# A causal convolution and a two-layer SiLU network on one core: transposes moved from the matmul engine to DMA, 192 channels packed as 128 + 128, a third PSUM buffer, and the second matmuls delayed by one chunk

## The chip, the cores and the metric

The kernel runs on one NeuronCore of a Trainium2 chip. The metric is the device time of one execution in microseconds (us). Most executions of one kernel agree within 0.3%. "Granted clock" is the PE clock in the profile, 1.00 at full speed. Engines are named as in the profile: PE is the matmul engine, PEld its weight loads, DVE the vector engine, ACT the scalar (activation) engine, SP the engine whose queue issues most DMAs.

## The reference, cut to what matters

```python
# x: (8, 4096, 192) f32, weight: (8 heads, 7 taps)
w = softmax(weight, axis=-1)
out = einsum('hk,bskhg->bshg', w, x_unf)     # causal 7-tap convolution along the sequence, per head of 24 channels
h = out.reshape(32768, 192) @ w_in           # (192, 2048)
g = h * (1 / (1 + exp(-beta * h)))           # beta: one number for each of the 2048 columns
return g @ w_out                             # (2048, 192)
```

## The kernel before

The 32768 tokens go in 32 chunks of 1024. The convolution wants channels on partitions, x comes with tokens on partitions, so x is cast to fp16, transposed on PE into PSUM (the memory that holds the results of the matmuls) and copied by DVE to SBUF (the on-chip memory that holds their operands). DVE then does 7 taps for each of two halves of 96 channels. "First matmuls" below are those that make `hpsum`, "second matmuls" those that make `opsum`.

```python
    ps_tr = ... bufs=2     # transposes, 2 KB a partition each
    ps_h  = ... bufs=2     # hpsum, 4 KB each
    ps_o  = ... bufs=2     # opsum, 1.5 KB each
    # ... weights are loaded and cast ...
    for c in range(nchunks):
        # ... 8 loads of x, 4 casts to fp16 on ACT ...
        for hh in range(2):
            tr = ps_tr.tile([128, NSUB // 2, 256], FP16)
            for si in range(NSUB // 2):
                s = hh * (NSUB // 2) + si
                nc.tensor.transpose(tr[0:DB, si, 0:SUB], x16[:, s, 0:DB], ident)
                nc.tensor.transpose(tr[0:DB, si, SUB:2 * SUB], x16[:, s, DB:D], ident)
            # ... two copies of tr into xt1 and xt2 on DVE ...
        # ... per half: tensor_scalar_mul, then 6 scalar_tensor_tensor on DVE; the last writes yt
        for fc in range(NFC):                          # 16 steps
            hpsum = ps_h.tile([128, CHUNK], FP32)
            # ... 4 first matmuls of 512 columns from win1/yt1 and win2/yt2 ...
            nc.scalar.activation(gt[:, fc, :], hpsum, AF.Silu, scale=beta_sb[:, fc:fc + 1])
        for sg in range(NSUB // 2):
            opsum = ps_o.tile([SUB, 2, D], FP32)
            # ... 2 x 16 second matmuls of 192 columns from gt and wout ...
            o_sb = opool.tile([SUB, 2, D], FP32)
            nc.scalar.copy(o_sb, opsum)
            # ... store ...
```

The instructions of each engine are put in order when the kernel is built, and this compiled order is not simply the program's. In the trace of the kernel before, second matmuls of a chunk are mixed into its own first ones, and transposes of later chunks stand at 485.9 us, ahead of a block of 98 second matmuls, and at 494.9 us, behind it.

## Time and profile before

| | before |
|---|---|
| median | 1036.39 us (12 runs) |
| PE, ACT, DVE busy | 904.2, 676.5, 544.3 us of 1033.7 |
| first and second matmuls a chunk | 64 of 512 columns, 128 of 192 columns |
| two chunks (485 to 547 us) | 62.3 us |
| dense PE time for one chunk (estimate, below) | 24.3 us |

From the page of the kernel before: busy time of each engine, the granted PE clock in 40 slices, and the chain of work that ended last.

```profile
PE 904.2 (87%) x6656; PEld 582.7 (56%) x6656; DVE 544.3 (53%) x719; ACT 676.5 (65%) x780; POOL 0.7 (0%) x6
...
PEclk9999999898998989989898998989989899998989
...
PE 68%; DVE 25%; ACT 4%; SPq 1%; DMA 1%; issue 0%; DVEq 0%; ACTq 0%
```

PE looks nearly full, but a quarter of the chain is DVE's: PE is held up at times. The granted clock dips too. The list of waits of the kernel before (who waited for whom, us in total, times, longest) says by what.

```profile
DVE xt L148 <- PE tr L146: 449.3, 17, 30.0
ACT o_sb L205 <- PE opsum L197: 175.9, 113, 2.2
...
ACT gt L188 <- PE hpsum L184: 130.5, 84, 8.3
PE hpsum L184 <- DVE yt L169: 99.7, 32, 10.0
```

DVE waits for PE's transposes, up to 30 us at a time, and PE then waits for DVE's convolution. Two engines wait for each other in turn. The PE timeline of the kernel before shows (start, us, engine, what, count; idle time before and what ended it in brackets):

```profile
501.71 1.01 PE L184 MATMUL hpsum<-yt,win 96*128 96x512 bf16 x2 [5.72 <-DVE yt L169]
502.91 4.29 PE L184 MATMUL hpsum<-yt,win 96*128 96x512 bf16 x10 [0.18 <-DVE yt L169]
```

After the wait of 5.72 us a first matmul takes about 430 ns, twice its later time; the granted clock is 0.50 from 501.7 to 504 us, 0.63 to 508 us and 1.00 after that (busy time by stretches). That is about 2.6 us lost each time (2.3 x 0.50 + 4.0 x 0.37). The trace has 15 such waits from 126 us on, one in every second chunk, so about 39 us in all, an estimate.

The next lines show two steps of an hpsum phase and, last, the block that ended the chunk before it.

```profile
534.24 1.02 PE L184 MATMUL hpsum<-yt,win 96*128 96x512 bf16 x4
535.10 0.41 PE L197 MATMUL opsum<-wout,gt 128*128 128x192 bf16 x3
535.47 1.02 PE L184 MATMUL hpsum<-yt,win 96*128 96x512 bf16 x4
536.33 0.25 PE L197 MATMUL opsum<-wout,gt 128*128 128x192 bf16 x1
536.47 1.02 PE L184 MATMUL hpsum<-yt,win 96*128 96x512 bf16 x4
...
522.91 8.26 PE L197 MATMUL opsum<-wout,gt 128*128 128x192 bf16 x98
```

Two steps take 2.23 us (534.24 to 536.47), 1.115 each, with 2 second matmuls a step on average. The other 98 of a chunk follow in a block at 82 ns each, 8.0 us. In such a block (523 to 531 us) ACT is busy for 2.6 of 8.0 us. At the same rate per column a first matmul takes about 215 ns, so PE's own work is 64 x 0.215 + 128 x 0.082 = 24.3 us a chunk, an estimate.

### The profile page before, as it was taken

How to read it: one execution, taken by the hardware profiler on the slowest of the kernel's cores; microseconds unless marked ns; L12 is line 12 of the kernel's file. 1: busy time of each engine (PE TensorE's matmuls, PEld its weight loads, DVE VectorE, ACT ScalarE, POOL GpSimd, SP SyncE). 2: the span in 40 equal slices, each digit the busy share in tenths (PEclk: the TensorE clock that was granted, in tenths of full speed). 3: DMA queues.
4: the chain of work that ended last, by engine and by line, in shares of the span. 5: the costliest groups of instructions: out<-in, count | busy, mean ns of one | idle time of the engine just before them, and what ended most of it. 6: DMA issues, size and time to landing. Idle time of an engine off the chain costs nothing.

```text
span 1033.7 us, 15639 instructions
## 1 busy us (share of the span) xinstructions
PE 904.2 (87%) x6656; PEld 582.7 (56%) x6656; DVE 544.3 (53%) x719; ACT 676.5 (65%) x780; POOL 0.7 (0%) x6
## 2 busy tenths in 40 slices
PE   1599799797998979799797997979899797997978
PEld 1266566365664656556465663656646465664655
DVE  6970653908448092661917538093571916529060
ACT  3777577674777747677575776747677474765735
POOL 0000000000000000000000000000000000000000
PEclk9999999898998989989898998989989899998989
DMA  6741301203021130301203021031200010010001
GB/s 170 195 125 32 92 21 48 56 31 93 31 62 31 32 92 32 85 16 37 79 31 93 23 62 39 31 92 32 62 2 31 31 32 31 16 32 16 31 31 32
DMA packets 77215, 54.52 MB, mean 53 GB/s; under 512 B 8792, under 2 KB 76376, under 8 KB 77144
## 3 DMA queue, kind: packets, MB, share of 16 engines
q1 hardware_dynamic: 77144, 53.52, 18.1%
q8 instruction: 52, 0.85, 0.3%
q14 instruction: 19, 0.16, 0.1%
HBM read 28.33 MB, written 25.17 MB: 52 GB/s over the span
## 4 chain that ended last, share of the span: by engine, by line
PE 68%; DVE 25%; ACT 4%; SPq 1%; DMA 1%; issue 0%; DVEq 0%; ACTq 0%
PE hpsum L184 46%; PE opsum L197 21%; DVE acc L169 18%; DVE yt L169 4%; ACT gt L188 3%; DVE acc L166 1%; DVE xt L148 1%; DVE xt L152 1%; SPq L121 1%; DMA x_sb<-in_x_dram 0%; DMA beta_sb<-in_moe_beta_dram 0%; PE tr L145 0%; PE tr L146 0%; ACT x L129 0%; DVE wout L112 0%
## 5 line engine op out<-in xcount | busy, mean ns | idle before, releaser
L188 ACT ACTIVATE gt<-hpsum,beta_sb 128x1024 bf16<-128x1024 f32 x512 | 552.0, 1113 | 148.1 <-PE hpsum L184 130.5
L184 PE MATMUL hpsum<-yt,win 96*128 96x512 bf16 x2048 | 559.2, 402 | 101.8 <-DVE yt L169 99.7
L197 PE MATMUL opsum<-wout,gt 128*128 128x192 bf16 x4096 | 422.7, 247 | 2.6 <-ACT gt L188 0.7
L197 PEld LDWEIGHTS <-gt 128*128 128x128 bf16 x4096 | 346.7, 98 | 105.2 <-ACT gt L188 19.8
L169 DVE SCALAR_TENSOR_TENSOR acc<-xt,wk,acc 96x1024 f16<-96x1024 f16 (+1 forms) x350 | 390.4, 1182 | 0.0
L184 PEld LDWEIGHTS <-win 96*128 96x128 bf16 x2048 | 205.5, 101 | 317.1 <-issue 158.9
L148 DVE COPY xt<-tr 96x512 f16<-96x512 f16 x64 | 26.5, 414 | 449.3 <-PE tr L146 449.3
L205 ACT COPY o_sb<-opsum 128x384 f32<-128x384 f32 x128 | 61.2, 478 | 178.2 <-PE opsum L197 175.9
L169 DVE SCALAR_TENSOR_TENSOR yt<-xt,wk,acc 96x1024 bf16<-96x1024 f16 (+1 forms) x70 | 80.3, 1182 | 0.0
L129 ACT CAST x<-x_sb 128x384 f16<-128x384 f32 x128 | 58.4, 511 | 21.3 <-DMA x_sb<-in_x_dram 17.1
L145 PE MATMUL tr<-ident,x 128*96 128x128 f16 x256 | 39.4, 231 | 21.1 <-ACT x L129 20.9
L145 PEld LDWEIGHTS <-x 128*96 128x96 f16 x256 | 31.8, 131 | 24.2 <-ACT x L129 23.9
L146 PE MATMUL tr<-ident,x 128*96 128x128 f16 x256 | 39.2, 230 | 0.0
L146 PEld LDWEIGHTS <-x 128*96 128x96 f16 x256 | 31.9, 132 | 0.3 <-issue 0.3
L166 DVE TENSOR_SCALAR acc<-xt,wk 96x1024 f16<-96x1024 f16 (+1 forms) x70 | 29.1, 452 | 0.0
L152 DVE COPY xt<-tr 96x512 f16<-96x512 f16 x64 | 26.2, 410 | 0.0
L101 ACT CAST win<-win_stage 96x512 bf16<-96x512 f32 x8 | 4.9, 617 | 2.6 <-DMA win_stage<-in_moe_w_in_dram 2.6
L112 DVE TENSOR_SCALAR wout<-wout_stage,rbeta 128x192 bf16<-128x192 f32 x16 | 4.7, 311 | 1.6 <-DMA wout_stage<-in_moe_w_out_dram 1.6
L137 DVE COPY xt<-xt 96x6 f16<-96x6 f16 x24 | 3.9, 161 | 0.0
L138 DVE COPY xt<-xt 96x6 f16<-96x6 f16 x24 | 3.8, 159 | 0.0
L80 ACT ACT_TABLE_LOAD x1 | 1.3, 1283 | 3.6 <-DMA wk<-in_weight_dram 3.6
L76 DVE TENSOR_REDUCE wmax<-wk 96x1 f32<-96x7 f32 x2 | 0.3, 156 | 3.3 <-DMA wk<-in_weight_dram 3.3
(20 smaller groups left out, 6.9 us busy)
## 6 DMA issues: line engine op xcount, KB each, us to landing
x_sb<-in_x_dram SPq DMA_DIRECT2D x256, 96.0 KB, 2.1
out_dram<-o_sb SPq DMA_DIRECT2D x128, 192.0 KB, 2.1
win_stage<-in_moe_w_in_dram SPq DMA_DIRECT2D x8, 192.0 KB, 3.0
wout_stage<-in_moe_w_out_dram SPq DMA_DIRECT2D x16, 96.0 KB, 2.2
wk<-in_weight_dram SPq DMA_DIRECT2D x2, 2.6 KB
beta_sb<-in_moe_beta_dram SPq DMA_DIRECT2D x1, 8.0 KB, 4.2
```

Of the source, the lines that this page charges most:

```text
L121: nc.sync.dma_start(out=x_sb[:, s, :], in_=x_flat[t0 + s * SUB:t0 + (s + 1) * SUB, :] .rearrange("(s p) d -> p s d", p=SUB)[:, 0, :],)
L129: nc.scalar.copy(x16[:, sl, :], x_sb[:, sl, :])
L145: nc.tensor.transpose(tr[0:DB, si, 0:SUB], x16[:, s, 0:DB], ident)
L146: nc.tensor.transpose(tr[0:DB, si, SUB:2 * SUB], x16[:, s, DB:D], ident)
L148: nc.vector.tensor_copy(xt1[:, base:base + HALF].rearrange("p (s t) -> p s t", s=NSUB // 2), tr[0:DB, :, 0:SUB],)
L152: nc.vector.tensor_copy(xt2[:, base:base + HALF].rearrange("p (s t) -> p s t", s=NSUB // 2), tr[0:DB, :, SUB:2 * SUB],)
L166: nc.vector.tensor_scalar_mul(acc[:, lo:lo + plen], xt[:, lo:lo + plen], wk[:, 0:1])
L169: nc.vector.scalar_tensor_tensor(out=(acc if k < K - 1 else yt)[:, lo:lo + plen], in0=xt[:, lo + k:lo + k + plen], scalar=wk[:, k:k + 1], ...
L184: nc.tensor.matmul(hpsum[:, hs], lhsT=win[:, fc * 128:(fc + 1) * 128], rhs=yt[:, hs], start=st, stop=not st,)
L188: nc.scalar.activation(gt[:, fc, :], hpsum, AF.Silu, scale=beta_sb[:, fc:fc + 1],)
L197: nc.tensor.matmul(opsum[:, si, :], lhsT=gt[:, fc, st * SUB:(st + 1) * SUB], rhs=wout[:, fc, :], start=(fc == 0), stop=(fc == NFC - 1),)
L205: nc.scalar.copy(o_sb, opsum)
```

## The change

Its intent is to take the transposes off PE and DVE, and to keep PE and ACT busy at the same time. It has four parts.

```diff
+    xstage = dpool.tile([NT, DP], FP16)                      # scratch in DRAM
-    ps_tr = ... bufs=2
-    ps_h  = ... bufs=2
+    ps_h  = ... bufs=3
 ...
     for c in range(nchunks):
         # ... loads and casts as before ...
+        for h in range(2):
+            nc.scalar.dma_start(out=xstage[<512 tokens>, 0:D], in_=x16[:, sl, :])
+        nc.sync.dma_start_transpose(out=xt1[:, XOFF:XOFF + CHUNK], in_=xstage[t0:t0 + CHUNK, 0:128])
+        nc.sync.dma_start_transpose(out=xt2[:, XOFF:XOFF + CHUNK], in_=xstage[t0:t0 + CHUNK, D - 128:D])
-        # 16 PE transposes and 4 copies from PSUM
 ...
         for fc in range(NFC):
             # ... first matmuls and activation as before, on 128 rows ...
+            if c > 0:
+                out_step(c - 1, gt_prev, fc)                 # 8 second matmuls of the chunk before
-        # all second matmuls of this chunk
+        gt_prev = gt
+    for step in range(16):
+        out_step(nchunks - 1, gt_prev, step)
```

The 192 channels are packed as channels 0 to 127 and 64 to 191. The second half's first 64 rows have zero taps and zero weights (cuts: the code that sets them up).

## The prediction

> **What bounds the kernel now.** A two-phase order on PE. The table of busy time gives PE 904 us (87%), ACT 677, DVE 544 of 1034. A chunk has 64 first matmuls (hpsum, 512 columns) and 128 second ones (opsum, 192 columns). In the timeline's dense stretches, at granted clock 1.00, 98 second matmuls take 8.03 us, 82 ns each; a 512-column one then costs about 215 ns (estimate, same rate per column). PE's floor is 64 x 0.215 + 128 x 0.082 = 24.3 us a chunk. Two chunks take 62.3 us (timeline, 485 to 547):
> 1. While hpsum is made, PE goes at ACT's pace: activations follow each other every 1.11 us, 17.8 us a chunk, with only 30 second matmuls in between. The other 98 follow, 8.1 us, ACT mostly waiting (list of waits: ACT o_sb for opsum, 176 us).
> 2. Every second chunk PE waits for the convolution (hpsum for DVE yt, 99.7 us, up to 10 us each), because transposes sit behind the 98-block; DVE waits 449 us for them. The chain of waits: PE 68%, DVE 25%.
> 3. 512 transposes on PE, about 55 ns each: 0.9 us a chunk. The clock falls to 0.87-0.90 around the gaps.
>
> **What the change does.** It removes the PE transposes (28 us) and DVE's PSUM copies (53 us), frees banks for a third hpsum buffer, and delays the second matmuls by one chunk, eight after each activation. A step is then 4 x 0.215 + 8 x 0.082 = 1.52 us of PE against 1.11 us of activation: ACT no longer paces PE. Packing 192 rows as 128 + 128 is neutral: durations go with columns.
>
> It adds, per chunk, two fp16 writes to DRAM issued from ACT and two DMA transposes of 256 KB. ACT: 17.8 + casts 1.75 + copies 1.9 = 21.5 us, plus about 1.5 for two issues (0.4 us each on SP here, plus stalls): 23, just under PE's 24.3. DVE: 12 x 1.2 + 2 x 0.45 + small copies = 15.5 us. DMA is 18% busy now. The Trainium skill, "Advanced Engine Details and Errata", X-Bar Transpose, expects 350-400 GB/s: 1.5 us for 512 KB. "VectorE: DVE Perf Modes", The three transpose paths, has 1309 ns for 128x128: 16 in series would be 21 us, barely under 24. No trace shows it yet; I guess 3 to 8 us each, hidden by buffering.
>
> **Sum.** Chunk 0 no longer streams in pieces; it is cast, written, read back and convolved: first full step near 50 us instead of 37. Then chunk 0, ACT-paced, 17.8; 31 chunks at 24.9 (24.3 plus 2% friction) 772; last second matmuls 10.5; end 4. Together 854 us. Nearly all gain comes from interleaving and the DVE wait; dropping PE transposes gives 0.9 us a chunk.
>
> **Prediction: 854 us, range 826 to 915; faster by over 2%: 0.93, within 2%: 0.03, slower: 0.04.**
>
> **What would show it.** Right: hpsum and opsum over 93% of the chain, 24.9 us a chunk, granted clock 0.98 or more, ACT waiting for PE, hpsum waiting for yt only at the start, DVE near 490 us busy. Wrong: hpsum waiting for ACT; DVE waiting for the transposing DMA throughout; SP blocked on transposes.
>
> **What would make it wrong.** Transposes above 12 us each, making DMA the bound (30 us a chunk would undo everything); SP's in-order queue, where a transpose waiting for its write holds up loads and stores; ACT stalling on its writes; a lower clock under dense load.

## The result, and the profile after

The kernel after takes 844.77 us (median of 8 runs, 843.29 to 846.12), against 1036.39 for before in the same rounds. The ratio is 0.8152 (95% interval 0.8144 to 0.8160).

From the page of the kernel after, the lines that answer to those of before:

```profile
PE 780.3 (93%) x6033; PEld 539.7 (64%) x6144; DVE 512.2 (61%) x593; ACT 669.4 (79%) x780; POOL 0.2 (0%) x4
...
PEclk9999999999999999999999999999999999999999
...
PE 92%; DMA 3%; DVE 2%; SPq 1%; issue 1%; ACT 1%; ACTq 0%
PE hpsum L229 51%; PE opsum L135 41%; DVE acc L214 1%; DMA wout_stage<-in_moe_w_out_dram 1%; DMA x_sb<-in_x_dram 1%; DVE yt L214 1%; DMA win_stage<-in_moe_w_in_dram 1%; DMA xt<-xstage 0%; DMA xstage<-x 0%; DVE wout L121 0%; DVE acc L210 0%;
```

The chain is now PE, 92%, and the mean granted clock is 1.00 (0.943 before). The list of waits of the kernel after:

```profile
DVE yt L214 <- PE hpsum L229: 160.1, 23, 21.9
ACT gt L233 <- PE hpsum L229: 104.1, 255, 0.9
DVE acc L210 <- DMA xt<-xstage: 63.8, 25, 4.8
...
PE hpsum L229 <- DVE yt L214: 50.4, 3, 37.7
```

DVE and ACT now wait for PE, and PE waits for the convolution 3 times, all at the start: one wait of 37.7 us before the first matmul and two more before 55 us. The timeline of the kernel after, in the middle and at the end:

```profile
480.30 1.03 PE L229 MATMUL hpsum<-yt,win 128*128 128x512 bf16 x4
481.16 0.82 PE L135 MATMUL opsum<-wout,gt 128*128 128x192 bf16 x8
481.82 1.03 PE L229 MATMUL hpsum<-yt,win 128*128 128x512 bf16 x4
482.69 0.82 PE L135 MATMUL opsum<-wout,gt 128*128 128x192 bf16 x8
...
828.64 11.23 PE opsum L135 x136
```

(The last line is from the chain in order of time.) A step takes 1.52 us and 16 of them 24.37, which is PE's own work with no friction at all. (111 of 2048 first matmuls are missing from this trace, so PE's busy time reads low and a stretch that shows 99% is full.) The profile's DMA issues (KB each, median us to landing; the second line has no KB) show the new transfers:

```profile
xstage<-x ACTq DMA_DIRECT2D x64, 192.0 KB, 2.8
...
xt<-xstage SPq DMA_TRANSPOSE x64, 3.5
```

The sum of the prediction against the trace, in us:

| term | predicted | measured |
|---|---|---|
| until chunk 0's 16 steps are through | 50 + 17.8 = 67.8 | about 74 |
| 31 chunks | 772 (24.9 each) | 755 (24.37 each), to 829.3 |
| last second matmuls and end | 14.5 | 14.2 |
| all | 854 | 843.5 profiled, 844.8 timed |

### The profile page after: what moved, and what is told of

It is laid out like the page before. It is cut to its first block, busy times and chain, and to the rows that moved or that the text cites. A ratio compares the mean times of both kernels' runs of the same rounds, so it can differ in the third digit from the quotient of the medians. Undisturbed runs are those within 1.5% of the kernel's fastest.

```text
span 843.5 us, 14627 instructions
## 1 busy us (share of the span) xinstructions
PE 780.3 (93%) x6033; PEld 539.7 (64%) x6144; DVE 512.2 (61%) x593; ACT 669.4 (79%) x780; POOL 0.2 (0%) x4
## 3 DMA queue, kind: packets, MB, share of 16 engines
q1 hardware_dynamic: 144751, 70.30, 33.4%
## 4 chain that ended last, share of the span: by engine, by line
PE 92%; DMA 3%; DVE 2%; SPq 1%; issue 1%; ACT 1%; ACTq 0%
PE hpsum L229 51%; PE opsum L135 41%; DVE acc L214 1%; DMA wout_stage<-in_moe_w_out_dram 1%; DMA x_sb<-in_x_dram 1%; DVE yt L214 1%; DMA win_stage<-in_moe_w_in_dram 1%; DMA xt<-xstage 0%; DMA xstage<-x 0%; DVE wout L121 0%; DVE acc L210 0%; ACT L233 0%; SPq L159 0%; ACT gt L233 0%; ACT x L167 0%
## 5 line engine op out<-in xcount | busy, mean ns | idle before, releaser
L233 ACT ACTIVATE gt<-hpsum,beta_sb 128x1024 bf16<-128x1024 f32 x512 | 569.3, 1119 | 123.5 <-PE hpsum L229 104.1
L229 PE MATMUL hpsum<-yt,win 128*128 128x512 bf16 x1937 | 515.2, 382 | 56.7 <-DVE yt L214 50.4
L135 PEld LDWEIGHTS <-gt 128*128 128x128 bf16 x4096 | 353.5, 98 | 119.2 <-issue 1.1
L214 DVE SCALAR_TENSOR_TENSOR acc<-xt,wk,acc 128x1024 f16<-128x1024 f16 (+1 forms) x350 | 395.7, 1187 | 1.6
L229 PEld LDWEIGHTS <-win 128*128 128x128 bf16 x2048 | 193.7, 98 | 180.7 <-issue 52.0
L214 DVE SCALAR_TENSOR_TENSOR yt<-xt,wk,acc 128x1024 bf16<-128x1024 f16 (+1 forms) x70 | 80.9, 1189 | 160.2 <-PE hpsum L229 160.1
L167 ACT CAST x<-x_sb 128x384 f16<-128x384 f32 x128 | 63.4, 517 | 30.2 <-DMA x_sb<-in_x_dram 28.9
L210 DVE TENSOR_SCALAR acc<-xt,wk 128x1024 f16<-128x1024 f16 (+1 forms) x70 | 31.5, 459 | 63.9 <-DMA xt<-xstage 63.8
L104 ACT CAST win<-win_stage 128x512 bf16<-128x512 f32 x4 | 2.5, 617 | 4.2 <-DMA win_stage<-in_moe_w_in_dram 4.1
L195 DVE COPY xt<-xt 128x6 f16<-128x6 f16 x24 | 4.1, 170 | 0.0
L192 DVE COPY xt<-xt 128x6 f16<-128x6 f16 x24 | 3.9, 165 | 0.0
```

The source lines that it names most:

```text
L104: nc.scalar.copy(win1[:, cs], win_stage)
L135: nc.tensor.matmul(opsum[:, si, :], lhsT=gt[:, fc, st * SUB:(st + 1) * SUB], rhs=wout[:, fc, :], start=(fc == 0), stop=(fc == NFC - 1),)
L167: nc.scalar.copy(x16[:, sl, :], x_sb[:, sl, :])
L192: nc.vector.tensor_copy(xt1[:, XOFF - PAD:XOFF], prev_xt1[:, XOFF + CHUNK - PAD:XOFF + CHUNK])
L195: nc.vector.tensor_copy(xt2[:, XOFF - PAD:XOFF], prev_xt2[:, XOFF + CHUNK - PAD:XOFF + CHUNK])
L210: nc.vector.tensor_scalar_mul(acc[:, lo:lo + plen], xt[:, base + lo:base + lo + plen], wk[:, 0:1])
```

## The experiments

Two of the change's parts can be taken apart: how the transposes are done, and where the second matmuls go. Whether the third buffer matters can be asked for each. This is the picture that the runs below give (medians, us):

| transposes | second matmuls after the chunk's own first ones | spread over the next chunk |
|---|---|---|
| on PE, compiled late, 2 hpsum buffers | 1036.6 (before) | 971.9 |
| on PE, one chunk ahead, 2 hpsum buffers | 901.4 | 857.7 |
| by DMA, 2 hpsum buffers | 923.3 | 848.4 |
| by DMA, 3 hpsum buffers | 881.2 | 844.8 (after) |

### Only the order

The kernel before, with the second matmuls taken from `out_step` as in the change; transposes stay on PE.

```diff
+            if c > 0:
+                out_step(c - 1, gt_prev, fc)
-        for sg in range(NSUB // 2):   # own second matmuls
```

> The kernel before with only the order changed: eight second matmuls of the previous chunk after each activation; transposes stay on PE, two hpsum buffers stay. Theory O (the order gives nearly all of the gain, as predicted): about 25.3 us a chunk (24.4 plus 0.9 of transposes), 860 to 890 us in all, and hpsum hardly waits for the convolution. Rival T (what matters is that transposes leave PE and DVE): the wait of DVE for the transposes and of PE for the convolution stays, 980 us or more. Rival B (the third hpsum buffer matters): 980 us or more too, with hpsum waiting for ACT.

Measured: 971.91 us, ratio 0.9379 (0.9361 to 0.9397). None of the theories had it: the order alone gives 65 us of the 192. From the list of waits and the timeline of this run:

```profile
DVE xt L177 <- PE tr L175: 384.6, 16, 34.7
...
PE hpsum L213 <- DVE yt L198: 62.8, 22, 10.0
```

```profile
514.72 0.22 PE L174 MATMUL tr<-ident,x 128*96 128x128 f16 x1
...
515.06 10.72 PE L126 MATMUL opsum<-wout,gt 128*128 128x192 bf16 x128
```

DVE still waits for transposes that stand late in PE's list, and PE for the convolution, as rival T expected of the waits. In the compiled order 128 second matmuls still stand in one block, once in two chunks, with no first matmuls beside them; in the other chunk they are spread, eight to a step. That the late convolution is why the block stays is a reading that no run tests alone.

### Only the DMA transposes, with two and with three hpsum buffers

The kernel after with the second matmuls put back after the chunk's own first ones, and `ps_h` at 2 or at 3.

```diff
-            if c > 0:
-                out_step(c - 1, gt_prev, fc)
+        for sg in range(NSUB // 2):   # own second matmuls, as before
-    ps_h ... bufs=3
+    ps_h ... bufs=2                   # first of the two runs only
```

> The kernel after with the order of before (all second matmuls after the chunk's own first ones) and two hpsum buffers: DMA transposes and packing alone. Theory O: little is gained over before, 980 us or more. Rival T: the waits of PE for the convolution go (about 4 us a chunk) and 0.9 us of transposes, so about 26.2 us a chunk, 880 to 910 us; the hpsum steps still come every 1.11 us.

> As the run with DMA transposes alone, but with three hpsum buffers as in the kernel after; only the order is that of before. Theory O (activations pace the hpsum phase at 1.11 us a step whatever the buffers): same as with two buffers. Rival B (the 1.11 us is the round trip of two buffers, 1.11 of activation plus 1.02 of matmuls plus signals over two): steps fall to about 1.03 us, a chunk takes 24.6 us, and the time is within 2% of the kernel after, 840 to 860 us.

Measured: 923.32 us (ratio 0.8918, 0.8899 to 0.8937) with two buffers, and 881.18 us (0.8501, 0.8488 to 0.8514) with three. So the DMA transposes alone give 113 us. The third buffer gives 42 more in this order. The first run lies above its expected 880 to 910 us: the chunk takes 25.9 us, a little under the expected 26.2, but the first 300 us are slower (below). In the second, the expected 840 to 860 us was missed mostly because the chunk takes 25.4 us, not 24.6. The ACT timelines show why, first with two buffers, then with three (time of a run of activations, count):

```profile
503.31 16.70 ACT L204 ACTIVATE gt<-hpsum,beta_sb 128x1024 bf16<-128x1024 f32 x15 [0.34 <-PE hpsum L200]
```

```profile
521.33 16.18 ACT L204 ACTIVATE gt<-hpsum,beta_sb 128x1024 bf16<-128x1024 f32 x16 [0.34 <-PE hpsum L200]
```

One activation alone takes 1.11 us. With two buffers they follow at (16.70 - 1.11) / 14 = 1.114 us, with three at (16.18 - 1.11) / 15 = 1.005. So 1.11 us was not ACT's pace. It is half the round trip of two buffers: 1.11 of activation, 1.02 of a group of four first matmuls, and about 0.1 that is left over make the 2.23 us of two steps. ACT's own pace, with the next operand waiting, is 1.005. The Trainium skill has this in "ScalarE: Activation LUTs", What ACT_TABLE_LOAD costs: "Back-to-back ACTIVATEs overlap by ≈ 93 ns". The 0.11 us between 1.11 and 1.005 is close to it. I could have read from it before predicting that a spacing of a full 1.11 us means waiting.

The PE blocks come every 25.92 us with two buffers and every 25.40 with three (starts of the long blocks, PE timelines of the two runs):

```profile
494.15 8.26 PE L213 MATMUL opsum<-wout,gt 128*128 128x192 bf16 x98
520.07 8.26 PE L213 MATMUL opsum<-wout,gt 128*128 128x192 bf16 x98
```

```profile
510.01 10.42 PE L213 MATMUL opsum<-wout,gt 128*128 128x192 bf16 x121
535.41 10.42 PE L213 MATMUL opsum<-wout,gt 128*128 128x192 bf16 x121
```

Half a microsecond a chunk is only about 17 of the 42 us. Most of the rest lies in the first 300 us: between 100 and 300 us PE is 89% busy with two buffers and 98% with three (busy time by stretches). In that stretch PE waited for activations 17.6 us with two buffers and 3.4 us with three (lists of waits). That fits a third buffer that bridges delays of ACT; no run isolates it. What is left over the kernel after, 1.03 us a chunk, goes with the order: the first matmuls go at ACT's pace, and ACT then stands mostly idle during the block.

### The kernel before with three hpsum buffers

```diff
-    ps_tr ... bufs=2      ps_h ... bufs=2      ps_o ... bufs=2
+    ps_tr ... bufs=1      ps_h ... bufs=3      ps_o ... bufs=1
```

> The kernel before with three hpsum buffers, paid for with one buffer less for the transposes and one less for opsum. Theory O: nothing gained, 1030 us or more, steps in the hpsum phase stay at 1.11 us. Rival B: steps fall to about 1.03 us, 1.4 us a chunk or 45 us in all, about 990 us, unless the single transpose and opsum buffers cost as much.

Measured: 1045.85 us, ratio 1.0093 (1.0078 to 1.0108), 0.9% slower, which is clear of the noise but within the 2% that count as the same. Theory O had the time right and the steps wrong. The steps did fall, as the round trip says (PE timeline of this run, 1.00 us from step to step), but PE paid for the buffers that were taken (list of waits of this run):

```profile
513.44 1.02 PE L184 MATMUL hpsum<-yt,win 96*128 96x512 bf16 x4
514.30 0.25 PE L197 MATMUL opsum<-wout,gt 128*128 128x192 bf16 x1
514.44 1.02 PE L184 MATMUL hpsum<-yt,win 96*128 96x512 bf16 x4
```

```profile
PE opsum L197 <- ACT o_sb L205: 59.0, 96, 0.9
PE hpsum L184 <- DVE yt L169: 51.5, 32, 10.0
```

With a single opsum buffer PE waits 59 us for its copy, and 51.5 us for the convolution remain. (The granted clock is 0.998 in this run, so a full clock alone does not make the kernel faster.) In the change, the third hpsum buffer of 4 KB a partition takes the room of the two transpose buffers of 2 KB. No run asked whether before could have had it beside all its other buffers.

### The kernel after with two hpsum buffers

```diff
-    ps_h ... bufs=3
+    ps_h ... bufs=2
```

> The kernel after with two hpsum buffers instead of three. Theory O' (with the second matmuls spread, a step is 1.52 us of PE, longer than the two-buffer round trip of 1.11 us): the third buffer is worth nothing here, 842 to 855 us, within 2% of the kernel after. Rival B (the third buffer is worth its 42 us in any order, as it was with the order of before): 880 us or more, with hpsum waiting for ACT.

Measured: 848.43 us, ratio 0.8189 (0.8174 to 0.8204), 0.4% over the kernel after. With the second matmuls spread, a step is 1.52 us of PE, longer than the 1.115 us to which two buffers held the steps before, half a round trip. The third buffer is worth 42 us in one order and 4 in the other.

### PE transposes, placed one chunk ahead

Two runs: the loop's front (load, transposes, convolution) becomes a function that is traced for chunk c+1 ahead of the matmuls of chunk c. No DMA transposes, no packing, two buffers. Loads, casts and the convolution move together with the transposes. The first run also has the second matmuls spread; the second is the kernel before with nothing else changed.

```diff
+    def front(c):            # load, cast, PE transposes, copies, convolution, as before
+        ...
+        return yt1, yt2
+    ys = front(0)
     for c in range(nchunks):
+        yt1, yt2 = ys
+        if c + 1 < nchunks:
+            ys = front(c + 1)
         # ... matmuls of chunk c ...
```

> PE transposes as in the kernel before, two hpsum buffers, second matmuls spread as in the kernel after, and the load, transposes and convolution of chunk c+1 traced ahead of the matmuls of chunk c, so that the compiled order puts the 16 transposes of a chunk between two chunks' matmuls, one chunk early. Theory P (what the DMA transposes gave was that the convolution no longer depends on a late place in PE's order; the 0.9 us of PE work a chunk is small): a chunk takes 24.4 + 0.9 = 25.3 us, the start is as short as before (37 us), together 845 to 870 us, and hpsum waits for yt only at the start. Rival T (the transposes and PSUM copies themselves cost the time on PE and DVE): 920 us or more, as the run with only the order changed (972) or little better.

> The kernel before with one thing changed: load, transposes and convolution of chunk c+1 are traced ahead of the matmuls of chunk c. Transposes stay on PE, two hpsum buffers, the second matmuls stay after the chunk's own first ones. Theory P (what the DMA transposes gave alone, 113 us, was the earlier place of the transposes): hpsum waits for yt only at the start, a chunk takes about 26.8 us, 905 to 930 us in all, as good as the run with DMA transposes alone (923). Rival T (taking the work off PE and DVE was needed): 980 us or more.

Measured: 857.68 us (ratio 0.8276, 0.8264 to 0.8289) with the second matmuls spread, and 901.37 us (0.8699, 0.8684 to 0.8713) in the order of before. The first lies in the range that theory P gave, the second 4 us below it. The placement alone gives 135 us, more than the DMA transposes alone (113). From the list of waits and the PE timeline of the second run, then the PE timeline of the first:

```profile
PE hpsum L192 <- DVE yt L169: 10.7, 2, 10.0
```

```profile
513.95 8.25 PE L205 MATMUL opsum<-wout,gt 128*128 128x192 bf16 x98
540.66 8.25 PE L205 MATMUL opsum<-wout,gt 128*128 128x192 bf16 x98
```

```profile
512.15 0.22 PE L173 MATMUL tr<-ident,x 128*96 128x128 f16 x1
...
513.04 1.03 PE L220 MATMUL hpsum<-yt,win 96*128 96x512 bf16 x4
513.91 0.82 PE L126 MATMUL opsum<-wout,gt 128*128 128x192 bf16 x8
```

The 16 transposes of a chunk take 0.89 us of PE (512.15 to 513.04), and PE waits for the convolution only at the start. The 135 us are nearly accounted for: PE's wait for the convolution falls from 99.7 to 10.7 us, and the granted clock is 1.00, which saves the 39 us or so of slow matmuls after those waits. So most of the 113 us was not the cost of the transposes but of where the compiled order had put them. Their own cost shows in the chunk, 26.71 us here against 25.92 with DMA transposes in the same order. The DMA run is slower in all because it starts later and loses time in its first 300 us. With the second matmuls spread, the DMA route saves 9 us over well-placed PE transposes with two buffers (848.4 against 857.7): about 28 us of PE work (32 x 0.89) less a later start. Full steps begin at 37.3 us with PE transposes and at 59.8 us with DMA transposes and two buffers, which leaves 6 of the 9 us.

### Each DMA transpose twice

```diff
         nc.sync.dma_start_transpose(out=xt1[...], in_=xstage[t0:t0 + CHUNK, 0:128])
+        nc.sync.dma_start_transpose(out=xt1[...], in_=xstage[t0:t0 + CHUNK, 0:128])
         nc.sync.dma_start_transpose(out=xt2[...], in_=xstage[t0:t0 + CHUNK, D - 128:D])
+        nc.sync.dma_start_transpose(out=xt2[...], in_=xstage[t0:t0 + CHUNK, D - 128:D])
```

> The kernel after with each DMA transpose issued twice (same data to the same place). Theory O' (transposes lie off the critical path; landing takes 3.5 us and a chunk has 24.4): within 1% of the kernel after, 840 to 853 us, DVE waits for the transposes longer. Rival D (the DMA transposes or the SP queue are near their limit): 870 us or more, with hpsum waiting for the convolution in every chunk.

Measured: 858.58 us, ratio 0.8292 (0.8274 to 0.8310), 1.6% over the kernel after. This missed both ranges. The stretches tell where the 14 us are (PE busy is the first number after the stretch's length; first the kernel after, then this run):

```profile
60.00:100.00 40.00, 39.74 (x253) 23.84 (x257) 39.92 (x44) 37.00 (x44) 0.00 (x0) 1.00 0.64 159
100.00:200.00 100.00, 99.26 (x777) 69.20 (x790) 99.86 (x105) 90.75 (x119) 0.00 (x0) 1.00 0.63 162
200.00:300.00 100.00, 99.20 (x772) 68.76 (x785) 64.69 (x67) 89.86 (x118) 0.00 (x0) 1.00 0.65 162
```

```profile
60.00:100.00 40.00, 34.10 (x212) 20.03 (x216) 39.92 (x43) 35.10 (x40) 0.00 (x0) 1.00 0.75 180
100.00:200.00 100.00, 94.58 (x715) 64.97 (x726) 91.59 (x98) 80.99 (x108) 0.00 (x0) 0.97 0.81 189
200.00:300.00 100.00, 99.20 (x774) 68.96 (x788) 67.29 (x69) 91.31 (x121) 0.00 (x0) 1.00 0.75 183
```

From 200 us on nothing changes: there the transposes are off the critical path, and doubling them is free. Before that DMA is 63 to 85% busy in the kernel after, with weights and x for several chunks ahead, and 75 to 84% here, and the delay reaches PE. Each transpose also holds SP's queue for 1.16 us; whether the DMA engines or that queue cost the 14 us is not separated. The run shows an activation released only by the landing of x, 6.3 us late, because its place in ACT's list is behind a write of cast x (near 138 us).

### A shorter start

Three runs from the kernel after. The first has chunk 0's convolution in one piece instead of four. The second also loads, casts, writes and transposes chunk 0 ahead of the weights, and loads the second weights after its convolution. The third also loads x with one DMA a chunk from chunk 1 on.

```diff
-        npieces = 4 if c == 0 else 1
+        npieces = 1                               # all three
+    first = load(0)                               # second and third: ahead of the weights
+        if c == 0: ... load and scale wout ...    # second and third: after chunk 0's convolution
-        for s in range(NSUB): nc.sync.dma_start(out=x_sb[:, s, :], ...)
+        nc.sync.dma_start(out=x_sb, ...)          # third, c > 0
```

> The kernel after with chunk 0's convolution in one piece, nothing else changed. If the 56 small DVE instructions set the start, it shortens by 6 to 9 us and the time falls to 836 to 839 us; if the loads set it, no change (843 to 846).

> The kernel after with a shorter start: chunk 0 is loaded, cast, written and transposed ahead of the weights, its convolution is in one piece (14 DVE instructions of up to 1.28 us instead of 56 small ones), and the second weights are scaled after it. If the rest stays at 24.4 us a chunk, the gain is that of the start alone: steady matmuls from about 32 to 40 us instead of 59, so 817 to 828 us. If the loads ahead of the weights only move the wait to the weights: 840 us or more.

> The run with the short start, with one DMA per chunk for x instead of eight from chunk 1 on. If the rest of the loss in the first 200 us comes from the SP queue's issue time (8 issues of 0.46 us a chunk) it falls to 822 to 828 us; if it comes from the DMA engines or from a cast that now waits for the whole chunk, 831 us or more.

Measured: 838.82 us (ratio 0.8093, 0.8080 to 0.8105), 831.32 us (0.8022, 0.8008 to 0.8036) and 827.25 us (0.7979, 0.7965 to 0.7992). In before, pieces let each part start as soon as its part of x was transposed (what they gave there, no run shows). When the whole chunk arrives at once they only cost DVE time: 256-column instructions take 0.48 us, 1024-column ones 1.28. The second run came out 3 us above its range: the first matmul comes at 31.1 us, but PE is 96% busy between 100 and 200 us against 99% in the kernel after. With one load for eight that stretch is 100% busy, so the loss was tied to the eight small loads of x. Whether SP's issue time or the spread of landings was it, is not separated. The third run lies in the range expected if SP's issue time was the loss, but it changes both. It starts as follows (PE timeline) and is the fastest kernel, 2.1% under the kernel after by the medians.

```profile
30.50 5.86 PE L245 MATMUL hpsum<-yt,win 128*128 128x512 bf16 x16 [30.50 <-DVE yt L224]
```

## Why the prediction was right, and where it was not

- **The floor and the step: right.** 1.52 us of PE a step was predicted and 1.52 measured. The granted clock is 1.00 and PE is 92% of the chain (over 93% was expected). The Trainium skill, "Perfetto Trace Analysis", Optimization Strategy, says that where the most-contended engine changes over time, "performance may be improved by interleaving those regimes". Here the regimes were an hpsum phase paced by buffers and ACT, and a block of PE alone; with the DMA transposes the interleaving is worth 36 us with three buffers and 75 with two.
- **"31 chunks at 24.9 (24.3 plus 2% friction)": the mis-sized term.** There is no friction; a chunk takes 24.37, so 31 chunks take 17 us less than predicted. In part the start made up for it: chunk 0 is through about 6 us later than predicted. That the two errors have opposite signs is luck. Predicting "near 50 us" left out that 56 small DVE instructions share DVE with the scaling of the second weights. The run with one piece shows 6 us of it.
- **"PE goes at ACT's pace: activations follow each other every 1.11 us": wrong mechanism, harmless for the sum.** The spacing was that of two hpsum buffers. ACT's pace is 1.005 us. This hid that the third buffer could matter (42 us in the order of before). In the order of after it is worth only 4 us, so the total was right anyway, by luck.
- **"Nearly all gain comes from interleaving and the DVE wait": right.** The order alone gives 65 us, ending the DVE wait alone 113 (by DMA) or 135 (by placement). Together, with two buffers, they give 188 by DMA, 10 more than the sum of the parts, and 179 by placement, 21 less. The prediction noted the lower clock around the gaps but did not say that it was part of the price of the wait: about 39 us, by the estimate above. "Dropping PE transposes gives 0.9 us a chunk" is confirmed at 0.89.
- **The DMA transposes, "3 to 8 us each, hidden by buffering": right in size and right after 200 us.** They landed in a median of 3.5 us. In the first 200 us the slack is thin, as doubling them shows.
- **ACT's load and its writes: right.** ACT is busy 669.4 us, 20.9 a chunk (21.5 were predicted without the issues). It waits for PE's first matmuls 255 times, 0.9 us at most; PE waits for an activation once, 3.3 us at the start.
- **Packing as neutral:** instructions of 96 and of 128 partitions take the same time in the two traces (1.27 to 1.28 us on DVE for 1024 columns). No run isolates the packing.

## What to carry to other kernels

Ask where in an engine's list an instruction stands before asking what it costs: 16 transposes of 0.89 us in all held up a chunk by 4 us (135 / 32), and tracing the loop's front, with them in it, one chunk earlier gave 135 us without moving them to another engine. A steady spacing equal to the length of one instruction can come from a buffer round trip as well as from a busy engine; compare it with that engine's back-to-back spacing. Once PE is dense, look at the first 200 us: here 17.5 us came off by convolving the first chunk in one piece (6), loading it ahead of the weights (7.5) and loading each later chunk with one DMA (4).

## What the Trainium skill lacked or had wrong

- "Advanced Engine Details and Errata", X-Bar Transpose, expects 350-400 GB/s and transposes as fast as plain DMAs. Doubling the 64 transposes of 256 KB raised the DMA engines' packet time on the main queue from 33.4% of 843.5 us to 43.9% of 857.0, that is 94.5 us or 1.48 us each on all 16 engines: an estimate of 177 GB/s. By the same measure the plain transfers of the kernel before ran at 286 GB/s (53.5 MB in 18.1% of 1033.7 us). The source rows were 256 B out of a pitch of 512 B, under other traffic whose packets may have slowed too; the section names no such condition. The measurement decides for this shape.
- "VectorE: DVE Perf Modes", The three transpose paths, has 1309 ns for 128x128 by DMA and nothing for larger ones. A transpose of 1024x128, eight such blocks, landed in a median of 3.5 us (3.0 to 6.0), so blocks do not add up in series. The page gives 390 ns for a PE transpose; here one lasts 0.22 us in the trace, and 16 follow each other at 55 ns, as 0.89 us for 16 shows.
- No section that was found says how long a transpose of this size from DRAM holds the issuing queue on this chip: it took 1.16 us on SP, a plain load of 96 KB 0.46 us.
- "Perfetto Trace Analysis", Optimization Strategy, looks for too few buffers in "consistent bubbles" on the engine that should be saturated. Here two PSUM buffers left no bubble on ACT, which the prediction took for the engine that set the pace: 15 activations stood end to end, at 1.114 us instead of 1.005.
